# A first load of 16 rows, and the norm at the head of VectorE, in an attention and MLP kernel bound by its loads

## The chip, the cores and the metric

The kernel runs on one core of a Trainium2 chip. The metric is the device time of one execution in microseconds; the time before is the median of 3 runs. The profile is of one further execution, whose own time is given beside its span. An engine in the profile is PE (TensorE, matrix products; PEld is its loading of weights), DVE (VectorE), ACT (ScalarE), POOL (GpSimd) or SP (SyncE, which issues the loads here). Data come from HBM, the memory of the chip, into SBUF, the on-chip memory of 128 partitions, by 16 DMA engines.

## What is computed

A layer for one decoded token of 8 sequences: x plus grouped-query attention over a cache plus an MLP with the Mish activation, both on the normed x.

```python
xn = layernorm(x)                        # x: 8 x 1 x 512
q = (xn @ wq).reshape(8, 1, 32, 128)     # 32 query heads, 8 key heads
k, v = repeat(k_cache, 4), repeat(v_cache, 4)   # caches: 8 x 8 x 8192 x 128
p = softmax(q @ k.T * 128 ** -0.5)
attention = (p @ v) @ wo
h = xn @ w1 + b1                         # 512 -> 1792
mlp = (h * tanh(softplus(h))) @ w2
out = x + attention + mlp
```

All is float32. The two caches are 537 MB of the 561 MB that are read; each byte of them is used once.

## The kernel before

The caches are worked off in 32 units (`UNITS`), one for each sequence and each pair of key heads. A unit has one load of keys and one of values, each 128 rows of 64 KB (8.39 MB), one row to a partition of the large tile `kv`. Values have one place in it, `V_AT`; the two places of keys, `K_AT`, take turns and overlap by a half. The first keys are put into the place of the values. The weights of four units' queries, `wq`, come into the tile `ws`; `w1` comes into `kv` from `W1_AT` on, where x, its centred copy `xc`, the squares and a permuted copy `xd` lie at first.

The program is written as a list of operations for each engine. A class, `Program`, records them in the order in which the code names them, finds which must wait for which, and emits each engine's list in that order; middle units are folded into loops on VectorE and TensorE. Every emitted instruction has the one line of the emitter (L378), so that the profile is read by tiles. `tell` and `take` are marks handed from a giver to a taker. SP's list is nearly only loads, issued in order; each load waits until the last readers and writers of its place are through.

The head of the program, ahead of the first unit, runs as follows. ACT's queue issues x (8 rows of 2 KB) and b1. SP issues `wq` (`load_q`, lines 495 to 498) and the first keys (`load_unit`, lines 500 to 508). VectorE clears four PSUM banks, then makes small constant matrices out of an identity matrix (`perm`, `gsum`, `mask`, `wide`, `dsel`, `fsel` and others, lines 524 to 568), and after them norms x (lines 571 to 585), with the squares and a square root on ScalarE. TensorE first multiplies x into the bank `A`, where the result is gathered; then it turns the normed x (`xn4`), and turns it once more in another order for the hidden layer (`xnT`). `project` multiplies `xn4` with `wq` in two halves, each copied by ScalarE to `qp` and turned into `M`. VectorE masks the queries, `spread` multiplies them out into `qr`, and `key_weights` makes the weights `wk` for the scores. `scores` takes `wk` and the keys (32 matmuls into the bank `S`), `softmax` finds the maximum and the exponentials, `turn` puts them in the order that `values` needs. `hidden` (18 matmuls with `w1` and `b1`) stands behind the first unit's `turn`.

Loads behind the head: `w1` and the second keys are issued ahead of the first projection in the code; the first values wait for the first scores, since they go into the place of the first keys; from there keys and values alternate.

Of the kernel before, what the change touches and what calls it, by code (L numbers as in the profile page):

```python
# [9 lines left out]
F32 = mybir.dt.float32  # L10
# [4 lines left out]
P = 128  # L15
# [44 lines left out]
K_AT = (ROW, ROW + ROW // 2)  # L60
W1_AT = ROW
W2_AT = 2 * ROW
PLACES = 2 * ROW + ROW // 2


# [360 lines left out]
def kernel(  # L426
# [68 lines left out]
    def load_q(m):  # L495

        rows = wq.rearrange("j p f -> (j p f)").rearrange("(m p f) -> m p f", m=NP, p=P)
        nc.sync.dma_start(ws, rows[m]).tell("wq")
# [14 lines left out]
    nc.scalar.dma_start(x_sb, x)  # L513
    b1_sb = kv[:G, W1_AT + 7168 : W1_AT + 7168 + FG]
    nc.scalar.dma_start(b1_sb, b1.rearrange("(g f) -> g f", g=G))
    load_q(0)
    k_t = {0: load_unit(kT, 0, V_AT)}
    w1_t = kv[:, W1_AT : W1_AT + W1R * W1F].rearrange("p (i f) -> p i f", i=W1R)


    make_identity(nc, ident)
    nc.gpsimd.memset(ones, 1.0)
    nc.gpsimd.memset(pt8, 0.0)
    for t in (H, O, M, A):
        nc.vector.memset(t, 0.0)
    for d in range(2):
        nc.vector.tensor_copy(
            perm.rearrange("p (d k c h) -> p d k c h", d=2, c=2, h=REP)[:, d],
# [2 lines left out]
    nc.vector.reduce_sum(  # L531
        gsum, ident.rearrange("p (x g q) -> p g x q", g=4, q=PP), axis=AX.XY
    )
    nc.vector.reduce_sum(mask, ident.rearrange("p (x d) -> p x d", x=NB), axis=AX.X)
    nc.vector.reduce_sum(bsel, ident.rearrange("p (g q) -> p q g", g=G), axis=AX.X)
    nc.vector.reduce_sum(
        isel, ident.rearrange("p (c t h) -> p t c h", t=TL, h=H2), axis=AX.XY
# [1 line left out]
    for d in range(2):  # L539
# [2 lines left out]
            ident.rearrange("p (c d k h) -> p d h c k", c=2, d=2, h=REP)[:, d],  # L542
            axis=AX.XY,
        )
    nc.vector.reduce_sum(
        wide[:, 0], ident.rearrange("p (g i) -> p g i", g=DG), axis=AX.X
    )
    nc.vector.tensor_copy(
        wide[:, 1:], wide[:, 0:1].to_broadcast([P, NB - 1, DG])
    )  # L550
    nc.vector.reduce_sum(dsel, ident.rearrange("p (g i) -> p i g", i=DI), axis=AX.X)
    nc.vector.reduce_sum(
        fsel, ident.rearrange("p (c h g) -> p h c g", h=2, g=2 * W1R), axis=AX.XY
    )
    nc.vector.reduce_sum(usel, ident.rearrange("p (q i) -> p i q", i=WOR), axis=AX.X)
    nc.vector.reduce_sum(
        qsel[:, :Q], ident.rearrange("p (q i) -> p q i", i=WOR), axis=AX.X
# [9 lines left out]
        .to_broadcast([G, 2, 2, B]),  # L567
    )


    st = const.tile([B, 8], F32, name="st")
    nc.vector.reduce_sum(st[:, 0:1], x_sb, axis=AX.X)
    nc.vector.tensor_scalar_mul(st[:, 1:2], st[:, 0:1], 1.0 / D)
    nc.vector.tensor_scalar(xc, x_sb, st[:, 1:2], None, op0=ALU.subtract)
    nc.scalar.activation(sq, xc, AF.Square, accum_out=st[:, 2:3])
    nc.vector.tensor_scalar(
        st[:, 3:4], st[:, 2:3], 1.0 / D, EPS, op0=ALU.mult, op1=ALU.add
    )
    nc.scalar.activation(st[:, 4:5], st[:, 3:4], AF.Sqrt)
    nc.vector.reciprocal(st[:, 5:6], st[:, 4:5])  # L580
    nc.vector.tensor_mul(st[:, 6:7], st[:, 5:6], st[:, 5:6])
    nc.vector.tensor_mul(st[:, 7:8], st[:, 6:7], st[:, 3:4])
    nc.vector.tensor_scalar(st[:, 6:7], st[:, 7:8], -0.5, 1.5, op0=ALU.mult, op1=ALU.add)
    nc.vector.tensor_mul(st[:, 4:5], st[:, 6:7], st[:, 5:6])
    nc.vector.tensor_scalar(xc, xc, st[:, 4:5], None, op0=ALU.mult)
    nc.tensor.matmul(A[:B, :], ident[:B, :B], x_sb, start=True, stop=False)
    for c in range(CC):
        nc.tensor.transpose(M[:, c * B : (c + 1) * B], xc[:, c::CC], ident[:B, :B])
    nc.vector.tensor_copy(xn4.rearrange("p c b -> p (c b)"), M[:, 0:32])
    xd = kv[:B, W1_AT + 3 * D : W1_AT + 5 * D].rearrange("p (i k) -> p i k", i=W1R)  # L590
    for h in range(2):
        nc.vector.tensor_copy(
            xd.rearrange("p i (c h g) -> p h i c g", c=CC, h=2)[:, h],
            xc.rearrange("p (c g i) -> p i c g", c=CC, i=W1R),
        )
    for i in range(W1R):
        nc.tensor.transpose(
            M[:, 32 + i * B : 32 + (i + 1) * B], xd[:, i], ident[:B, :B]
        )
    for h in range(2):  # L600
        nc.vector.tensor_scalar(
            xnT[:, :, h],
            M[:, 32 : 32 + W1R * B].rearrange("p (i b) -> p i b", i=W1R),
            fsel[:, h : h + 1],
            None,
            op0=ALU.mult,
        )

    def project(m, qp):

        nc.tensor.take("wq")
        w = ws.rearrange("p (c f) -> p c f", c=CC)
        for d in range(2):
            for c in range(CC):
                nc.tensor.matmul(
                    H[:B, :],
                    xn4[:, c, :],
                    w[:, c, d * 512 : (d + 1) * 512],
                    start=(c == 0),
                    stop=(c == CC - 1),  # L620
                )
            nc.scalar.copy(qp[:B], H[:B]).tell("qp")
            nc.tensor.take("qp")
            for h in range(REP):
                at = 192 + (d * REP + h) * B
                made = nc.tensor.transpose(
                    M[:, at : at + B], qp[:B, h * DH : (h + 1) * DH], ident[:B, :B]
                )
        made.tell("tq")
        qT = ws[:, 2 * BW : 2 * BW + H2 * B]  # L630
        nc.vector.take("tq")
        nc.vector.tensor_scalar_mul(qT, M[:, 192 : 192 + H2 * B], DH**-0.5).tell("q")
        return qT
# [47 lines left out]
    def scores(j, k, first, part):  # L681

        if part == 0:
            nc.tensor.take("wk", f"k{j % 2}")
        w = wk
        lo = 0 if first else DI // 2
        kk = k.rearrange("p (i c f) -> p i c f", i=DI, c=HALF)
        for n in range(DI // 2):
            i = lo + n
            for c in range(HALF):  # L690
                made = nc.tensor.matmul(
                    S[64 * c : 64 * (c + 1), :],
                    w[:, i].rearrange("p d k h -> p (d k h)"),
                    kk[:, i, c, :],
                    start=(part == 0 and n == 0),
                    stop=(part == 1 and n == DI // 2 - 1),
                )
        if part == 1:
            made.tell("s")

    def softmax(j):
        nc.vector.take("s")
        nc.vector.relay()
        nc.vector.tensor_reduce(nm, S, axis=AX.X, op=ALU.max, negate=True).tell("nm")
        nc.tensor.take("nm")
        nc.tensor.transpose(M[:1, 0:P], nm, ident).tell("mt")
        nc.vector.take("mt")
        row = M[:1, 0:P].rearrange("p (c d k h) -> p d h c k", c=2, d=2, h=REP)
        for d in range(2):
            low_max = nc.vector.tensor_reduce(nr[:, d], row[:, d], axis=AX.XY, op=ALU.min)  # L710
        low_max.tell("nr")
        nc.vector.take("nr")
        for c in range(2):
            wide_max = nc.vector.tensor_copy(
                nx[:, c],
                nr.rearrange("p d (o h) -> p d o h", o=1).to_broadcast([1, 2, NH * G, REP]),
            )
        wide_max.tell("nx")
        nc.tensor.take("nx")
        nc.tensor.transpose(  # L720
            M[:, 128:129], nx.rearrange("p c d k h -> p (c d k h)"), ident[:1, :1]
        ).tell("xt")
        nc.vector.take("xt")
        nc.vector.tensor_copy(nmx, M[:, 128:129])
        nc.scalar.activation(es[j % 2], S, AF.Exp, bias=nmx, accum_out=l).tell("e")
# [97 lines left out]

    hp = H[:, :FG]

    def hidden(w1_t, b1_sb):
        for i in range(W1R):
            for n in range(2):
                nc.tensor.matmul(
                    hp[Q * n : Q * n + 2 * B, :],  # L830
                    xnT[:, i].rearrange("p h b -> p (h b)"),
                    w1_t[:, i, n * FG : (n + 1) * FG],
                    start=(i == 0),
                    stop=False,
                )
        for n in range(2):
            nc.tensor.matmul(
                hp[Q * n : Q * n + 2 * B, :],
                gsel[:, n].rearrange("p h b -> p (h b)"),
                b1_sb,  # L840
                start=False,
                stop=True,
            )
        for e in range(2):
            nc.vector.tensor_copy(
                hid[64 * e : 64 * (e + 1)], hp[:64, FG // 2 * e : FG // 2 * (e + 1)]
            )
# [85 lines left out]
    def down(lo, hi, w):  # L933
# [8 lines left out]
            )  # L942


    nc.sync.dma_start(
        kv[:, W1_AT : W1_AT + W1R * W1F],
        w1.rearrange("j p f -> (j p f)").rearrange("(p f) -> p f", p=P),
    )
    qT = project(0, es[0])
    k_t[1] = load_unit(kT, 1, K_AT[1])  # L950
    mask_queries(qT)
    spread()
# [4 lines left out]
    for j in range(UNITS):  # L957
# [14 lines left out]
        elif j > 0:  # L972
            k_t[j + 1] = load_unit(kT, j + 1, K_AT[(j + 1) % 2])
        scores(j, k, j % 2 == 0, 1)
        softmax(j)
        if b == 0 and j > 0:
            with nc.only("sums"):
                sums()
# [15 lines left out]
            load_q(j // B + 1)  # L994
        if more and b == MAKE_Q:
            with nc.only("make"):
                qT = project(j // B + 1, es[(j + 1) % 2])
                mask_queries(qT)
        turn(j, late)
        if j == 0:  # L1000
            hidden(w1_t, b1_sb)
        if j > 0:
            merge(j - 1)
    sums()
# [86 lines left out]
```

## Time and profile before

| | before |
|---|---|
| median of 3 runs | 1303.69 us (1303.64 to 1304.04) |
| time of the profiled execution | 1303.81 us |
| its span, first to last instruction | 1302.0 us |
| busy: PE, DVE, ACT, POOL | 912.2, 399.5, 43.1, 1.7 us |
| read from HBM | 561.01 MB |
| mean rate over the span | 431 GB/s |

Rows of a timeline begin with the start and the length in microseconds, then have engine, line, operation, output<-inputs, and shapes; in square brackets stands how long the engine was idle ahead of it and what ended that. Rows of stretches have the borders, then the busy time of each engine, the granted clock of TensorE as a share, the mean busy share of the DMA engines and the rate in GB/s. A transfer that is under way at a border is counted to one side, so that in short stretches the share can pass 1.

### The profile page before, as it was taken

How to read it: one execution, taken by the hardware profiler on the slowest of the kernel's cores; microseconds unless marked ns; L12 is line 12 of the kernel's file. 1: busy time of each engine (PE TensorE's matmuls, PEld its weight loads, DVE VectorE, ACT ScalarE, POOL GpSimd, SP SyncE). 2: the span in 40 equal slices, each digit the busy share in tenths (PEclk: the TensorE clock that was granted, in tenths of full speed). 3: DMA queues.
4: the chain of work that ended last, by engine and by line, in shares of the span. 5: the costliest groups of instructions: out<-in, count | busy, mean ns of one | idle time of the engine just before them, and what ended most of it. 6: DMA issues, size and time to landing. Idle time of an engine off the chain costs nothing. (4 is left out here: it accounts for less than half of the span.)

```text
span 1302.0 us, 11473 instructions
## 1 busy us (share of the span) xinstructions
PE 912.2 (70%) x4570; PEld 297.8 (23%) x4570; DVE 399.5 (31%) x874; ACT 43.1 (3%) x104; POOL 1.7 (0%) x8
## 2 busy tenths in 40 slices
PE   4877767668766668775678666677576667666667
PEld 1222222222222222222222222222222222222121
DVE  3332233431333331233321333322333331333431
ACT  2000000000000000000000000000000000000000
POOL 0000000000000000000000000000000000000000
PEclk9899778898788788888887877798887798788788
DMA  9999999999999999999999999999999999999998
GB/s 400 452 422 441 427 437 433 435 433 431 439 427 443 425 445 425 443 425 445 425 443 427 443 427 441 429 435 433 433 437 433 435 429 441 427 443 425 443 418 351
DMA packets 11555, 561.22 MB, mean 431 GB/s; under 512 B 1292, under 2 KB 1552, under 8 KB 1944
## 3 DMA queue, kind: packets, MB, share of 16 engines
q1 hardware_dynamic: 11520, 561.06, 99.6%
q8 instruction: 6, 0.10, 0.0%
q14 instruction: 5, 0.04, 0.0%
q10 hardware_dynamic: 24, 0.02, 0.0%
HBM read 561.01 MB, written 0.07 MB: 431 GB/s over the span
## 5 line engine op out<-in xcount | busy, mean ns | idle before, releaser
L378 PE MATMUL s<-kv,wk 128*64 128x512 f32 x2048 | 515.7, 667 | 226.2 <-PEq L365 226.2
L378 PEld LDWEIGHTS s<-kv,wk 128*64 128x64 f32 x2048 | 174.5, 154 | 550.0 <-issue 550.0
L378 PE MATMUL o<-kv,pt 128*32 128x512 f32 x2048 | 268.1, 683 | 22.7 <-PEq L365 22.3
L378 DVE TENSOR_REDUCE nm<-s 128x1 f32<-128x512 f32 x32 | 22.1, 692 | 479.5 <-DVEq L365 479.5
L378 PEld LDWEIGHTS o<-kv,pt 128*32 128x32 f32 x2048 | 81.5, 123 | 183.1 <-issue 182.7
L378 DVE TENSOR_SCALAR os<-o,isel 128x128 f32<-128x128 f32 x32 | 11.2, 351 | 287.7 <-DVEq L365 287.7
L378 DVE STREAM_TRANSPOSE tr<-x 128x512 f32<-128x512 f32 x128 | 80.0, 682 | 1.3 <-DVEq L365 1.3
L378 DVE TENSOR_TENSOR wk<-qr,mask 128x512 f32<-128x512 f32 x64 | 61.8, 1007 | 8.9 <-DVEq L365 6.4
L378 DVE SCALAR_TENSOR_TENSOR pt<-tr,gsum,y 64x256 f32<-64x256 f32 x128 | 56.2, 479 | 5.2
L378 ACT ACTIVATE e<-s,nmx 128x512 f32<-128x512 f32 x32 | 22.0, 687 | 1046.1 <-DVE nmx L378 1046.1
L378 DVE SCALAR_TENSOR_TENSOR y<-tr,gsum,y 128x512 f32<-128x512 f32 x64 | 48.3, 755 | 9.4
L378 DVE SCALAR_TENSOR_TENSOR os<-o,isel,os 128x128 f32<-128x128 f32 x96 | 33.7, 351 | 14.1 <-DVEq L365 0.3
L378 PE MATMUL x<-e,perm 128*128 128x512 f32 x64 | 36.5, 653 | 1.4 <-PEq L365 1.3
L378 PE MATMUL m<-ident,nm 128*1 128x128 f32 x32 | 8.6, 269 | 32.2 <-PEq L365 32.2
L378 PE MATMUL h<-ws,xn 128*8 128x512 f32 x64 | 30.5, 622 | 0.0
L378 PE MATMUL m<-ident,nx 1*128 1x1 f32 x32 | 6.4, 200 | 34.2 <-PEq L365 34.2
L378 PE MATMUL t<-ident,os 128*128 128x128 f32 x32 | 9.6, 299 | 26.6 <-PEq L365 26.6
L378 DVE TENSOR_SCALAR y<-tr,gsum 128x512 f32<-128x512 f32 x32 | 24.1, 754 | 1.2
L378 DVE TENSOR_REDUCE nr<-m 1x4 f32<-1x64 f32 x64 | 11.0, 207 | 18.1 <-DVEq L365 18.1
L378 PEld LDWEIGHTS m<-ident,nm 128*1 128x1 f32 x32 | 2.5, 79 | 59.5 <-issue 59.5
L378 PEld LDWEIGHTS x<-e,perm 128*128 128x128 f32 x64 | 10.0, 192 | 24.1 <-issue 23.7
L378 PEld LDWEIGHTS t<-ident,os 128*128 128x128 f32 x32 | 4.5, 140 | 46.6 <-issue 46.6
(91 smaller groups left out, 154.1 us busy)
## 6 DMA issues: line engine op xcount, KB each, us to landing
ws<-in_wq SPq DMA_DIRECT2D x4, 2048.0 KB, 32.6
kv<-in_wo SPq DMA_DIRECT2D x4, 2048.0 KB, 24.4
kv<-in_w SPq DMA_DIRECT2D x1, 3584.0 KB, 22.0
kv<-in_w SPq DMA_DIRECT2D x2, 1024.0 KB, 32.0
kv<-in_w SPq DMA_DIRECT2D x2, 512.0 KB, 33.8
kv<-in_kT SPq DMA_DIRECT2D x32, 29.1
kv<-in_v SPq DMA_DIRECT2D x32, 29.4
kv<-in_w SPq DMA_DIRECT2D x1, 384.0 KB, 34.7
```

The lines of the kernel that those rows point to most:

```text
L378: ins = getattr(engine, op.method)(*[here(x) for x in op.args], **{k: here(x) for k, x in op.kw.items()})
```

## The change

Four things are changed in the head.

The first keys' load is cut in two on SP: 16 rows (`HEAD_ROWS`) are issued first, then `wq`, then the other 112 rows. TensorE's first score matmul takes the mark `k0` twice, once for each part. `w1` and the second keys are recorded behind the projection, no longer ahead of it.

SP's list, before and now; rows name the tile, the tensor that is loaded and the rows by elements of 4 bytes. Before:

```order
L378 DMA ws<-in_wq 128x4096
L378 DMA kv<-in_kT 128x16384
L378 DMA kv<-in_w 128x7168 [waits at_tensor]
L378 DMA kv<-in_kT 128x16384
L378 DMA kv<-in_v 128x16384 [waits past_vector]
```

Now:

```order
L379 DMA kv<-in_kT 16x16384
L379 DMA ws<-in_wq 128x4096
L379 DMA kv<-in_kT 112x16384
L379 DMA kv<-in_w 128x7168 [waits at_tensor]
L379 DMA kv<-in_kT 128x16384
L379 DMA kv<-in_v 128x16384 [waits past_vector]
```

One load has become two around `wq`; `w1` and the second keys have kept their places in the list, but `w1` waits for another instruction of TensorE.

VectorE norms x ahead of nearly all the constants. ScalarE takes a square root of one element of the identity at the start, so that its table is there.

VectorE from its start; `st` holds the sums of the norm, `kv<-kv,st` are steps on x itself, `m` and `h` are banks. Before:

```order
L378 MEMSET h 128x512
L378 MEMSET o 128x512
L378 MEMSET m 128x512
L378 MEMSET a 128x512
L378 COPY perm<-ident 128x64 x2
L378 TENSOR_REDUCE gsum<-ident 128x4
L378 TENSOR_REDUCE mask<-ident 128x16
L378 TENSOR_REDUCE bsel<-ident 128x32
```

Now:

```order
L379 MEMSET m 128x512
L379 TENSOR_REDUCE st<-kv 8x1
L379 TENSOR_SCALAR st<-st 8x1
L379 TENSOR_SCALAR kv<-kv,st 8x512
L379 MEMSET h 128x512
L379 TENSOR_REDUCE dsel<-ident 128x16
L379 TENSOR_SCALAR st<-st 8x1
L379 TENSOR_REDUCE wide<-ident 128x8
L379 RECIPROCAL st<-st 8x1
```

The norm stood behind some twenty rows of constants and is now at the second row, with constants between its steps and behind it.

TensorE makes both halves of the first projection in two banks, turns x for the hidden layer while ScalarE copies, and only then turns the queries; the matmul of x into `A` comes behind that. The 18 matmuls of the hidden layer are spread over the first softmax.

TensorE up to the first scores (`s`); `e_90` and `e_91` hold the copied queries. Before:

```order
L378 MATMUL a<-kv,ident 8x512
L378 MATMUL m<-ident,kv 128x8 x12
L378 MATMUL h<-ws,xn_82 8x512 x4
L378 MATMUL m<-ident,e_90 128x8 x4
L378 MATMUL h<-ws,xn_82 8x512 x4
L378 MATMUL m<-ident,e_90 128x8 x4
L378 MATMUL h<-ws,wide 128x512
L378 MATMUL y<-ws,wide 128x512
L378 MATMUL s<-kv,wk 64x512 x32
```

Now:

```order
L379 MATMUL m<-ident,kv 128x8 x4
L379 MATMUL h<-ws,xn_82 8x512 x4
L379 MATMUL y<-ws,xn_82 8x512 x4
L379 MATMUL x<-ident,kv 128x8 x8
L379 MATMUL m<-ident,e_90 128x8 x4
L379 MATMUL m<-ident,e_91 128x8 x4
L379 MATMUL a<-kv,ident 8x512
L379 MATMUL h<-ws,wide 128x512
L379 MATMUL y<-ws,wide 128x512
L379 MATMUL s<-kv,wk 64x512 x32
```

The matmul `a<-kv,ident`, the last reader of x, moved from the first row to behind the projection.

The diff, cut to its core:

```diff
+HEAD_ROWS = 16
...
-    load_q(0)
-    k_t = {0: load_unit(kT, 0, V_AT)}
+    k_t = {0: kv[:, V_AT : V_AT + ROW]}
+    k_rows = kT[:NB].rearrange("j p f -> (j p f)").rearrange("(p f) -> p f", p=P)
+    nc.sync.dma_start(k_t[0][:HEAD_ROWS], k_rows[:HEAD_ROWS]).tell("k0")
+    load_q(0)
+    nc.sync.dma_start(k_t[0][HEAD_ROWS:], k_rows[HEAD_ROWS:]).tell("k0")
...
-    for t in (H, O, M, A):
-        nc.vector.memset(t, 0.0)
+    st = const.tile([B, 8], F32, name="st")
+    nc.scalar.activation(st[:, 0:1], ident[:B, :1], AF.Sqrt)
+    nc.vector.memset(M, 0.0)
+    nc.vector.reduce_sum(st[:, 0:1], x_sb, axis=AX.X)
...
-    nc.tensor.matmul(A[:B, :], ident[:B, :B], x_sb, start=True, stop=False)
...
-    def project(m, qp):
+    def project(m, qps, banks, fill=None):
...
+        products(0)
+        if fill is not None:
+            products(1)
+            fill()
+            turned(0)
+        else:
+            turned(0)
+            products(1)
+        turned(1).tell("tq")
...
         if part == 0:
             nc.tensor.take("wk", f"k{j % 2}")
+            if j == 0:
+                nc.tensor.take("k0")
...
+    qT = project(0, es, (H, Y), turn_x)
+    nc.tensor.matmul(A[:B, :], ident[:B, :B], x_sb, start=True, stop=False)
     nc.sync.dma_start(
         kv[:, W1_AT : W1_AT + W1R * W1F],
         w1.rearrange("j p f -> (j p f)").rearrange("(p f) -> p f", p=P),
     )
-    qT = project(0, es[0])
     k_t[1] = load_unit(kT, 1, K_AT[1])
...
-        softmax(j)
+        if j == 0:
+            softmax(j, hidden)
+            hidden(4, 6)
+        else:
+            softmax(j)
...
         if j == 0:
-            hidden(w1_t, b1_sb)
+            hidden(6, W1R)
```

More of the change, by code (lines that the diff above doesn't have):

```diff
@@ L523 @@
     nc.gpsimd.memset(pt8, 0.0)
-    for t in (H, O, M, A):
-        nc.vector.memset(t, 0.0)
+    st = const.tile([B, 8], F32, name="st")
+    nc.scalar.activation(st[:, 0:1], ident[:B, :1], AF.Sqrt)
+    nc.vector.memset(M, 0.0)
+    nc.vector.reduce_sum(st[:, 0:1], x_sb, axis=AX.X)
+    nc.vector.tensor_scalar_mul(st[:, 1:2], st[:, 0:1], 1.0 / D)
+    nc.vector.tensor_scalar(xc, x_sb, st[:, 1:2], None, op0=ALU.subtract)
+    nc.scalar.activation(sq, xc, AF.Square, accum_out=st[:, 2:3])
+    nc.vector.memset(H, 0.0)
+    nc.vector.reduce_sum(dsel, ident.rearrange("p (g i) -> p i g", i=DI), axis=AX.X)
+    nc.vector.tensor_scalar(
+        st[:, 3:4], st[:, 2:3], 1.0 / D, EPS, op0=ALU.mult, op1=ALU.add
+    )
+    nc.scalar.activation(st[:, 4:5], st[:, 3:4], AF.Sqrt)
+    nc.vector.reduce_sum(
+        wide[:, 0], ident.rearrange("p (g i) -> p g i", g=DG), axis=AX.X
+    )
+    nc.vector.reciprocal(st[:, 5:6], st[:, 4:5])
+    nc.vector.tensor_mul(st[:, 6:7], st[:, 5:6], st[:, 5:6])
+    nc.vector.tensor_mul(st[:, 7:8], st[:, 6:7], st[:, 3:4])
+    nc.vector.tensor_scalar(st[:, 6:7], st[:, 7:8], -0.5, 1.5, op0=ALU.mult, op1=ALU.add)
+    nc.vector.tensor_mul(st[:, 4:5], st[:, 6:7], st[:, 5:6])
+    nc.vector.tensor_scalar(xc, xc, st[:, 4:5], None, op0=ALU.mult)
+    for c in range(CC):
+        nc.tensor.transpose(M[:, c * B : (c + 1) * B], xc[:, c::CC], ident[:B, :B])
+    nc.vector.tensor_copy(xn4.rearrange("p c b -> p (c b)"), M[:, 0:32])
+    nc.vector.tensor_copy(
+        wide[:, 1:], wide[:, 0:1].to_broadcast([P, NB - 1, DG])
+    )
+    nc.vector.reduce_sum(mask, ident.rearrange("p (x d) -> p x d", x=NB), axis=AX.X)
+    xd = kv[:B, W1_AT + 3 * D : W1_AT + 5 * D].rearrange("p (i k) -> p i k", i=W1R)
+    for h in range(2):
+        nc.vector.tensor_copy(
+            xd.rearrange("p i (c h g) -> p h i c g", c=CC, h=2)[:, h],
+            xc.rearrange("p (c g i) -> p i c g", c=CC, i=W1R),
+        )
+    nc.vector.reduce_sum(
+        fsel, ident.rearrange("p (c h g) -> p h c g", h=2, g=2 * W1R), axis=AX.XY
+    )
+    nc.vector.memset(A, 0.0)
+    nc.vector.memset(O, 0.0)
     for d in range(2):
@@ L533 @@
     )
-    nc.vector.reduce_sum(mask, ident.rearrange("p (x d) -> p x d", x=NB), axis=AX.X)
     nc.vector.reduce_sum(bsel, ident.rearrange("p (g q) -> p q g", g=G), axis=AX.X)
@@ L544 @@
         )
[L545 to L554, printed above, removed]
     nc.vector.reduce_sum(usel, ident.rearrange("p (q i) -> p i q", i=WOR), axis=AX.X)
@@ L568, with products @@
     )
[L571 to L585, printed above, removed]
-    nc.tensor.matmul(A[:B, :], ident[:B, :B], x_sb, start=True, stop=False)
[L587 to L607, printed above, removed]
-    def project(m, qp):
+    def project(m, qps, banks, fill=None):
         nc.tensor.take("wq")
         w = ws.rearrange("p (c f) -> p c f", c=CC)
-        for d in range(2):
+        def products(d):
             for c in range(CC):
                 nc.tensor.matmul(
-                    H[:B, :],
+                    banks[d][:B, :],
                     xn4[:, c, :],
@@ L621, in project, with turned @@
                 )
-            nc.scalar.copy(qp[:B], H[:B]).tell("qp")
+            nc.scalar.copy(qps[d][:B], banks[d][:B]).tell("qp")
+        def turned(d):
             nc.tensor.take("qp")
@@ L626, in project @@
                 made = nc.tensor.transpose(
-                    M[:, at : at + B], qp[:B, h * DH : (h + 1) * DH], ident[:B, :B]
+                    M[:, at : at + B], qps[d][:B, h * DH : (h + 1) * DH], ident[:B, :B]
                 )
-        made.tell("tq")
+            return made
+        products(0)
[7 more added lines that the diff above has]
+        turned(1).tell("tq")
         qT = ws[:, 2 * BW : 2 * BW + H2 * B]
@@ L699, in scores, with softmax @@
             made.tell("s")
-    def softmax(j):
+    def softmax(j, fill=lambda lo, hi: None):
         nc.vector.take("s")
@@ L704, in softmax @@
         nc.vector.tensor_reduce(nm, S, axis=AX.X, op=ALU.max, negate=True).tell("nm")
+        fill(0, 2)
         nc.tensor.take("nm")
@@ L718, in softmax @@
         wide_max.tell("nx")
+        fill(2, 4)
         nc.tensor.take("nx")
@@ L824, with hidden @@
     hp = H[:, :FG]
-    def hidden(w1_t, b1_sb):
-        for i in range(W1R):
+    def hidden(lo, hi):
+        for i in range(lo, hi):
             for n in range(2):
@@ L835, in hidden @@
                 )
+        if hi < W1R:
+            return
         for n in range(2):
@@ L942, in down, with turn_x @@
             )
+    def turn_x():
+        for i in range(W1R):
+            nc.tensor.transpose(X[:, i * B : (i + 1) * B], xd[:, i], ident[:B, :B])
+        for h in range(2):
+            nc.vector.tensor_scalar(
+                xnT[:, :, h],
+                X[:, : W1R * B].rearrange("p (i b) -> p i b", i=W1R),
+                fsel[:, h : h + 1],
+                None,
+                op0=ALU.mult,
+            )
+    qT = project(0, es, (H, Y), turn_x)
+    nc.tensor.matmul(A[:B, :], ident[:B, :B], x_sb, start=True, stop=False)
     nc.sync.dma_start(
@@ L996 @@
             with nc.only("make"):
-                qT = project(j // B + 1, es[(j + 1) % 2])
+                qT = project(j // B + 1, [es[(j + 1) % 2]] * 2, (H, H))
                 mask_queries(qT)
```

## The prediction

> **What bounds the kernel now.** I read the strip of forty slices first, then the chain of work that ended last, then single stretches of the span.
>
> ```profile
> DMA  9999999999999999999999999999999999999998
> 1263.61 34.75 DMA kv<-in_w
> 1298.40 0.74 PE h L378 x15
> 1299.16 0.29 DVE os L378
> ```
>
> The first row is the mean busy share of the 16 DMA engines in each fortieth of the span, in tenths: full everywhere. The other three (start, length, what) are the end of the chain: nearly 35 us of waiting for one load, then about 1 us of work on it. Busy engines do not prove that none of them waits, so I cut the span where the loads begin and end.
>
> ```profile
> core 0: us, PE busy (x) PEld busy (x) DVE busy (x) ACT busy (x) POOL busy (x), PEclk, DMA share, GB/s
> 1.80:1.98 0.18, 0.00 (x0) 0.00 (x0) 0.18 (x1) 0.15 (x1) 0.18 (x2) 1.00 0.19 68
> 2.00:3.00 1.00, 0.00 (x0) 0.00 (x0) 0.89 (x3) 1.00 (x1) 0.70 (x1) 1.00 1.08 217
> 3.00:4.00 1.00, 0.70 (x1) 0.10 (x2) 1.00 (x7) 0.11 (x1) 0.00 (x0) 1.00 0.78 295
> 4.00:5.00 1.00, 1.00 (x2) 0.00 (x0) 0.97 (x7) 0.00 (x0) 0.00 (x0) 1.00 0.99 426
> 27.00:1294.00 1267.00, 894.92 (x4464) 292.84 (x4468) 388.67 (x837) 37.93 (x96) 0.00 (x0) 0.84 1.00 434
> 1294.00:1302.00 8.00, 4.23 (x72) 1.32 (x64) 0.29 (x1) 0.58 (x1) 0.00 (x0) 0.93 0.33 124
> ```
>
> The last two columns matter. From 27 to 1294 us the DMA share is 1.00 at 434 GB/s, with no hole; all engines of computation have slack (TensorE is busy 895 of 1267 us). Before that, two microseconds carry little: at 2 to 3 and 3 to 4 us the rate is 217 and 295. So the time is one sum: when the loads start, plus bytes over rate, plus a tail of some 4 us behind the last byte. An edit matters only if it moves the start, lowers the rate, or lets the queue run empty. The span is 1302.0 us, the profiled execution 1303.81, which is 0.12 over the median of 1303.69; I sum against 1303.81.
>
> **The change part by part.** First, does the queue stay full when the order of the head is turned over?
>
> ```profile
> 0.90 0.59 ACTq L378 DMA_DIRECT2D kv<-in_x  x1
> 0.95 0.38 SPq L378 DMA_DIRECT2D ws<-in_wq  x1
> 1.39 0.42 SPq L378 DMA_DIRECT2D kv<-in_kT  x1
> 14.40 0.33 SPq L378 DMA_DIRECT2D kv<-in_w  x1
> 14.77 0.43 SPq L378 DMA_DIRECT2D kv<-in_kT  x1
> 49.92 0.33 SPq L378 DMA_DIRECT2D kv<-in_v  x1
> 71.28 0.33 SPq L378 DMA_DIRECT2D kv<-in_kT  x1
> ws<-in_wq SPq DMA_DIRECT2D x1, 2048.0 KB, 7.6
> kv<-in_w SPq DMA_DIRECT2D x1, 3584.0 KB, 22.0
> ```
>
> These are the issues (start, length), and for two of them KB and us to landing. wq is 2.10 MB, each load of keys or values 8.39 MB (128 rows of 64 KB), w1 3.67 MB. With a start at 2.0 and 0.8 us lost in the ramp, wq and the first keys keep the engines busy until 2.8 + 10.49 MB / 434 GB/s = 27.0 us; w1 and the second keys until 54.8; the first values until 74.1. The next issues come at 14.4, 49.9 and 71.3: early each time, by 12.6, 4.9 and 2.8 us.
>
> In the changed kernel w1 must wait for more of TensorE's row, since x and its copies lie where w1 lands and their last reader is now the 8x512 matmul behind the projection; the second keys stand behind w1 on SP. The chain up to there:
>
> ```profile
> 6.29 0.67 DVE L378 TENSOR_REDUCE st<-kv 8x1 f32<-8x512 f32 x1
> 8.41 1.28 ACT L378 ACT_TABLE_LOAD   x1
> 12.06 0.19 DVE L378 COPY xn<-m 128x32 f32<-128x32 f32 x1 [0.73 <-PE m L378]
> 3.29 1.87 PE L378 MATMUL a<-kv,ident 8*8 8x512 f32 x2 [3.29 <-DVE a L378]
> 13.35 1.02 PE L378 MATMUL m<-ident,kv 8*128 8x8 f32 x8 [1.33 <-DVE kv L378]
> 14.29 5.33 PE L378 MATMUL h<-ws,xn 128*8 128x512 f32 x8
> 20.69 3.60 PE L378 MATMUL h<-ws,xn 128*8 128x512 f32 x8
> 25.05 0.38 PE L378 MATMUL m<-ident,e 8*128 8x8 f32 x4 [0.76 <-PEq L365]
> 33.36 16.38 PE L378 MATMUL s<-kv,wk 128*64 128x512 f32 x64 [3.00 <-PEq L365]
> ```
>
> The norm now takes 12.25 - 6.29 = 5.96 us, a table load of 1.28 included. Moved to the head of VectorE it starts when x is there (by 3.29, when the matmul on x ran) and when the early square root is through, at about 3.4; the constants that stood ahead of it go behind it, and the second table load leaves the chain. xn is then ready at 3.4 + 5.96 - 1.28 = 8.1 instead of 12.25. The two memsets and reductions put among the norm's steps lie in its waits for ScalarE. wq now comes one packet later per engine: landed at 0.95 + 7.6 + 1.05 MB / 434 (2.4) = 11.0. So the projection starts at 11.0, not 14.29. Its two products take 5.33 + 3.60, the eight turns of x 1.02, the two turns of queries 0.76, the matmul on x 1.87: w1 is issued at 23.6, still 3.4 us ahead of the end of the queue at 27.0, and the second keys right behind. Data follow an issue after about 1 us (0.95 to 2.0). So the later w1 costs nothing, with 2.4 us to spare; each microsecond beyond that would cost one. The scores then wait for both loads of k0 rather than for the weights; the weights come some 3.7 us sooner (the last turn of queries ends at 11.0 + 10.7 = 21.7, not 25.4), so where k0 is on time v0 and k2 are issued that much sooner and gain slack, and where k0 is late the whole queue is late with it. All the rearranged work on VectorE, TensorE and ScalarE is thus worth **nothing**: the full queue hides it. w1's parts of the hidden layer now stand between the steps of the first softmax; w1 lands 8.5 us behind k0, inside the 16.38 us of scores.
>
> What is left is the queue itself. **Start.** The ramp at 2 to 4 us lacks 217 + 139 KB, 0.82 us at 434. [...] Between 0 and -0.8 us; I take the middle, -0.4. The extra issue (0.4 us on SP) and its completion packets lie under the first packets, at nothing.
>
> **First load (T1).** 16 rows of 64 KB go to partitions 0 to 15 alone. At full rate that is 1.05 MB / 434 = 2.4 us, and costs nothing, as these bytes were to be moved anyhow. But no big load in this trace is narrower than 128 partitions, and 434 GB/s over 128 partitions may be a limit of the engines (27 each) or of the places that take the data (3.4 for each partition). If the rate went by partitions, 16 of them would take 54 GB/s: 19.3 us, +16.9, and wq and all else would stand behind it in every engine's queue. These are the ends. The nearest row is the stretch 1.80 to 1.98: there only x is under way, on 8 partitions, at 68 GB/s, 8.5 for each partition. At that, 16 partitions take 136 GB/s: 7.7 us, **+5.3**. I take it, being the only narrow load seen; it is a stretch of start-up, so a loose guide.
>
> [...]
>
> **Third load (T2).** 112 rows, seven for each engine, 16.9 us at 434. [...] If all goes on at an engine's own pace: +0. If the rate follows the share of partitions, 112/128 of 434 gives 19.3 us, +2.4. If every packet shares its place with another: +16.9. Between 2.4 and 16.9, far apart and with no row nearer, I take the geometric middle, **+6.4**; it goes with T1, since both come from a limit on the side that takes the data.
>
> Sum: 1303.8 + 5.3 + 6.4 - 0.4 = **1315.1**, say 1315.
>
> **The rivals.** (a) *Narrow loads run at full pace*: the limit is the engines' 27 GB/s each. For it: 434 in the long stretch whatever the load. Then T1 and T2 are nothing and the time is 1303.8 - 0.4 = 1303.4 (1303.0 to 1304.0): not slower. It decides as soon as the first load is done by about 5 us. The same time comes out if the change doesn't do what it says, that is if the 16 rows go to few engines and those get fewer of the 112: each still has eight rows of k0. [...] (b) *Lockstep*: the 112 rows are dealt out so that all engines always write 16 neighbouring rows, seven times over; then each step costs what the first load costs: 8 x 5.3 = 42, 1346. Against it: loads of 128 rows show no such crowding. (c) *The queue runs empty* since w1 is late: it needs the projection's chain to slip by over 2.4 us with T1 at nothing; it would cost 1 to 3 us, 1304.4 to 1306.4.
>
> **How the numbers follow.** Forecast 0.55, (a) 0.34, (b) 0.07, (c) 0.04. The long stretch cannot tell engines from partitions; I lean to the partitions because the one narrow load seen moved at 68 where eight engines at 27 would give 217. The forecast's own range is 1306 (T1 and T2 near their low ends) to 1323 (T1 16.9 with T2 2.4). The range takes in (a) and these: 1302.9 to 1323, leaving out (b) and a tenth of the forecast's cases, where both terms are high. Runs of this kernel tell about 0.2%, 2.6 us, from no change. Faster by that: 0.03, taken out of (a), as the whole ramp holds only 0.8 us. Within it: the rest of (a), 0.31, and 0.03 of (c): 0.34. Slower: the forecast, (b) and the rest of (c): 0.63.
>
> **What would show it.** Forecast: DMA rate far under 434 between 3 and 10 us, wq landing after 14 us rather than 11, a rate under 434 until some 38 us, then 434 as before. (a): 430 from 3 us on and w1 issued near 23.6. (b): a low rate until 60 us and more. (c): a stretch near 27 us with an empty queue. Wrong above all if the places that take data have room for one engine per partition.

## The result, and the profile after

The changed kernel takes 1324.03 us (median of 4 runs, 1323.57 to 1324.47) against 1303.74 before (by now also 4 runs): 20.3 us slower, a ratio of 1.0156 with a 95% interval of 1.0143 to 1.0168. The time lies 1 us above the range of the prediction. The profiled execution took 1323.98 us, with a span of 1322.2.

The strip of forty slices of the changed kernel: the busy share of the DMA engines in tenths, and the rate in GB/s.

```profile
DMA  9999999999999999999999999999999999999998
GB/s 247 336 439 421 436 440 428 432 442 426 436 440 426 434 440 436 426 438 438 426 436 438 430 432 440 428 434 442 426 434 440 428 434 438 438 426 436 439 420 347
```

The first of these rows is the same as before and would hide everything: the engines are busy from the first slice on. The second row has the answer. In the first two slices (66 us) the rate is 247 and 336 where it was 400 and 452; from the third to the last but one both stay between 418 and 445. So a busy share near 1 does not mean full pace. Cut at the borders of the loads:

```profile
core 0: us, PE busy (x) PEld busy (x) DVE busy (x) ACT busy (x) POOL busy (x), PEclk, DMA share, GB/s
2.00:11.30 9.30, 0.65 (x4) 0.55 (x4) 6.59 (x25) 2.22 (x5) 0.70 (x1) 1.00 1.03 131
11.30:16.60 5.30, 0.00 (x0) 0.00 (x0) 1.59 (x8) 0.00 (x0) 0.00 (x0) 1.00 0.84 352
16.60:46.00 29.40, 13.24 (x38) 3.48 (x38) 3.85 (x6) 3.60 (x5) 0.00 (x0) 0.83 1.03 254
46.00:1314.00 1268.00, 886.71 (x4464) 291.32 (x4464) 386.71 (x834) 35.47 (x93) 0.00 (x0) 0.85 1.00 433
```

The stretch of the first load has 131 GB/s (a part of it is wq's first packets), that of wq (128 rows again) 352 (without those), that of the 112 rows 254, and everything behind has 433. The packet records of the trace (start, length and size of each transfer) say the same: each of the 16 rows took 7.9 to 9.2 us, where a packet of 64 KB took 2.42 us in the kernel before, while wq's packets came down to 0.61 us, as before. At 434 the 112 rows would have been through in 16.9 us; they take some 30. The issues and landings of the changed kernel say the same; in the last three rows the last number is us from issue to landing, of the 16 rows, of wq, and of the 112 rows.

```profile
0.95 0.39 SPq L379 DMA_DIRECT2D kv<-in_kT  x1
1.40 0.41 SPq L379 DMA_DIRECT2D ws<-in_wq  x1
1.86 0.63 SPq L379 DMA_DIRECT2D kv<-in_kT  x1
29.28 0.34 SPq L379 DMA_DIRECT2D kv<-in_w  x1
...
65.46 0.33 SPq L379 DMA_DIRECT2D kv<-in_v  x1
85.94 0.33 SPq L379 DMA_DIRECT2D kv<-in_kT  x1
...
kv<-in_kT SPq DMA_DIRECT2D x1, 11.8
...
ws<-in_wq SPq DMA_DIRECT2D x1, 2048.0 KB, 16.4
...
kv<-in_kT SPq DMA_DIRECT2D x1, 47.6
```

The engines of computation, in the timeline of the changed kernel:

```profile
8.02 0.19 DVE L379 COPY xn<-m 128x32 f32<-128x32 f32 x1 [0.74 <-PE m L379]
...
17.96 5.77 PE L379 MATMUL h<-ws,xn 128*8 128x512 f32 x8 [9.97 <-PEq L366]
28.23 1.02 PE L379 MATMUL a<-kv,ident 8*8 8x512 f32 x2
49.62 15.66 PE L379 MATMUL s<-kv,wk 128*64 128x512 f32 x64 [17.47 <-PEq L366]
```

The norm does what it was moved for: xn is ready at 8.2 us, not 12.25. But the projection then waits 10 us for wq, and the scores 17.5 us for the keys. At the other end the chain is as it was, 35.30 us of waiting for the last load against 34.75:

```profile
1283.20 35.30 DMA kv<-in_w
```

### The profile page after: what moved, and what is told of

It is laid out like the page before. It is cut to its first block, busy times and chain, and to the rows that moved or that the text cites. A ratio compares the mean times of both kernels' runs of the same rounds, so it can differ in the third digit from the quotient of the medians.

```text
span 1322.2 us, 11475 instructions
## 1 busy us (share of the span) xinstructions
PE 903.9 (68%) x4570; PEld 296.7 (22%) x4570; DVE 399.5 (30%) x874; ACT 42.1 (3%) x104; POOL 1.7 (0%) x8
## 5 line engine op out<-in xcount | busy, mean ns | idle before, releaser
L379 PE MATMUL h<-ws,xn 128*8 128x512 f32 x56 | 27.4, 635 | 10.0 <-PEq L366 10.0
## 6 DMA issues: line engine op xcount, KB each, us to landing
ws<-in_wq SPq DMA_DIRECT2D x4, 2048.0 KB, 33.8
```

The source lines that it names most:

```text
L379: ins = getattr(engine, op.method)(*[here(x) for x in op.args], **{k: here(x) for k, x in op.kw.items()})
```

## The experiments

Theory at the outset: all of the loss lies in the two loads that are narrower than 128 partitions, on the side that takes the data. Rivals: the new order of the head has a share in it; narrow loads are slow for their source, for their number of rows, or as they come first.

**Which half of the change.** One kernel keeps everything but the split of the first keys, one has nothing but the split.

```diff
 # e1_rest_only: the changed kernel
-    k_t = {0: kv[:, V_AT : V_AT + ROW]}
...
-    nc.sync.dma_start(k_t[0][:HEAD_ROWS], k_rows[:HEAD_ROWS]).tell("k0")
     load_q(0)
-    nc.sync.dma_start(k_t[0][HEAD_ROWS:], k_rows[HEAD_ROWS:]).tell("k0")
+    k_t = {0: load_unit(kT, 0, V_AT)}
...
-            if j == 0:
-                nc.tensor.take("k0")
 # e2_split_only: the kernel before
+    k_t = {0: kv[:, V_AT : V_AT + ROW]}
...
+    nc.sync.dma_start(k_t[0][:HEAD_ROWS], k_rows[:HEAD_ROWS]).tell("k0")
     load_q(0)
-    k_t = {0: load_unit(kT, 0, V_AT)}
+    nc.sync.dma_start(k_t[0][HEAD_ROWS:], k_rows[HEAD_ROWS:]).tell("k0")
...
+            if j == 0:
+                nc.tensor.take("k0")
```

> The changed kernel with the first keys in one load of 128 rows behind wq, as before; all the rest of the change stays. Theory (the loss is all in the two narrow loads): 1303.3 to 1303.9 us, no change against 1303.7, with wq landed near 9 us and w1 issued near 22 us, ahead of the end of the queue at 27. Rival (a good part of the 20 us comes from the order of the head, as w1 and the second keys are issued at 29 instead of 14 us): 1306 us or more, with a stretch near 27 us in which the DMA engines stand idle.

> The kernel before with nothing but the split load (16 rows, wq, 112 rows). Theory: the whole loss, 1323 to 1325 us, with the 112 rows at about 250 GB/s as in the changed kernel. Rival (order of the head matters): clearly under 1322 us.

Without the split: 1303.77 us (11 runs) against 1303.82, ratio 1.0 (0.9991 to 1.0009). With the split alone: 1324.02 (4 runs), ratio 1.0154 (1.0138 to 1.0171), with 250 GB/s in the stretch from 16.6 to 46 us, where the changed kernel has 254. The split is the whole loss; the new order of the head is worth nothing that can be measured, either way. A stretch of e1_rest_only, and its issues of w1 and of the first values:

```profile
4.00:27.00 23.00, 13.39 (x42) 3.97 (x42) 11.43 (x38) 4.53 (x8) 0.00 (x0) 0.97 1.00 434
```

```profile
19.48 0.33 SPq L379 DMA_DIRECT2D kv<-in_w  x1
...
44.37 0.33 SPq L379 DMA_DIRECT2D kv<-in_v  x1
```

w1 is issued 5 us later than before (19.5; 22 was expected) and the first values 5.5 us earlier, and neither shows, as the queue is full on both sides of them (434 GB/s from 27 to 1294 us as well).

**The same split, cut the other way.** The first load has the same 1.05 MB, but an eighth of the columns of all 128 rows.

```diff
 # e3_columns: the changed kernel
-    nc.sync.dma_start(k_t[0][:HEAD_ROWS], k_rows[:HEAD_ROWS]).tell("k0")
+    nc.sync.dma_start(k_t[0][:, : ROW // 8], k_rows[:, : ROW // 8]).tell("k0")
     load_q(0)
-    nc.sync.dma_start(k_t[0][HEAD_ROWS:], k_rows[HEAD_ROWS:]).tell("k0")
+    nc.sync.dma_start(k_t[0][:, ROW // 8 :], k_rows[:, ROW // 8 :]).tell("k0")
```

> The changed kernel, but the first keys are cut by columns and not by rows: first 128 rows of 2048 elements (the same 1.05 MB), then wq, then 128 rows of the other 14336. Theory (only the narrow set of partitions costs): 1303.5 to 1304.2, no change against before, the 20 us gone. Rival (two loads for one, or wq in second place, cost): over 1306.

It takes 1303.43 us (10 runs) against 1303.58, ratio 0.9998 (0.9989 to 1.0008): no difference. So neither the further load nor wq's second place costs anything. This is the way to have a piece of the keys first, and it does not beat the kernel before by an amount that can be told: what it could win is the ramp of the start alone, 0.8 us at 434 GB/s.

**The narrow loads by themselves.** The kernel before gets one load more ahead of wq, into the place of the second keys, which overwrite it later. The result stays what it was; there is 1.05 MB more to move (7.34 MB in p112), worth 2.4 us (16.9) at 434 GB/s. The probes of eight rows have half of the 1.05 MB; the estimate for them is 2.4 us all the same, for one packet of 64 KB (2.42 us in the kernel before) on each of eight engines. The rows come from the start of the first keys unless the table says otherwise (p112: rows 16 to 127).

```diff
 # the kernel before; the slices of the probes stand in the table
+    k_rows = kT[:NB].rearrange("j p f -> (j p f)").rearrange("(p f) -> p f", p=P)
+    spare = kv[:, K_AT[1] : K_AT[1] + ROW]
+    nc.sync.dma_start(spare[0:16], k_rows[0:16])
     load_q(0)
```

> The kernel before with one load more ahead of wq: the first 16 rows of the keys into partitions 0 to 15 of the place of the second keys, which are loaded over it later. At full rate the 1.05 MB cost 2.4 us: 1306.1. Theory (neighbouring partitions share a way in): the first load takes as long as in the changed kernel, 2.4 + 6.6 = 9.0 us more than before: 1312.7. Rival (the slow first load there was start-up or wq's place behind it): 1306 to 1308.

> The same as p16_step1, same 16 rows of HBM, but into partitions 0, 7, 14 and so on to 105. Theory (which partitions take the data decides, neighbours share a way in): well under p16_step1, with packets of mostly 2.4 us and the longest about 4.8: 1306 to 1309 us. Rival (a load of 16 rows is slow for its source or for its number of rows, or the rate goes by the number of partitions, 16 here as there): as p16_step1, 1312.7 us or more. [...]

> The kernel before with one load more ahead of wq: rows 16 to 127 of the first keys into partitions 16 to 127 of the place of the second keys. Theory (the third load of the change is slow by itself, without the first or wq around it): 7.34 MB in about 30 us as there, 1334. At an engine's full pace 16.9 us, 1320.7; by the share of partitions 19.3, 1323.1. Rival (it was slow there since the first load had put the engines out of step): 1321 to 1324.

> As p16_step7, with the same partitions 0, 7 to 105, but the rows of HBM are 0, 7 to 105 as well, 448 KB apart and not 64. Theory (the side that takes the data decides): 1308.2 as there. Rival (neighbouring rows of HBM are in each other's way): 1306.2.

> [...]

> As p16_step7, but into partitions 18, 25, 32 and so on to 123. [...]

> [...] Rival (a load of fewer than 128 rows pairs engines and places badly however they lie, or the step decides): 1308.3 as with start 0.

> [...]

> The kernel before with one load more ahead of wq: 8 rows of keys (64 KB each) into partitions 0, 4, 8 to 28. If each of eight engines takes one row at its full pace, these engines are 2.4 us later than before: 1306.2. The load into 16 partitions seven apart cost 4.5 us, twice the full pace on all 16 engines. [...]

> As p8_own, but into partitions 4, 8 to 32, one group further. [...]

> [...]

> [...] Time 1306.4 to 1308.5.

Each of these was run once. The rate is that of the stretch that is read below. The extra time is against the run of the kernel before beside it.

| probe | partitions | GB/s, 5.3 to 6.6 us | us to landing | time, us | extra, us |
|---|---|---|---|---|---|
| p16_step1 | 0:16 | 0 | 11.9 | 1312.86 | 9.0 |
| p16_step8 | 0:121:8 | 0 | 7.9 | 1308.65 | 5.0 |
| p16_step7 | 0:106:7 | 0 | 7.6 | 1308.25 | 4.4 |
| p16_src7 | 0:106:7, rows of HBM 0:106:7 | 67 | 8.2 | 1308.50 | 4.9 |
| p16_from10 | 10:116:7 | 0 | 8.0 | 1308.51 | 4.7 |
| p16_from18 | 18:124:7 | 346 | 8.9 | 1308.45 | 4.8 |
| p16_from11 | 11:117:7 | 407 | 5.6 | 1306.69 | 2.9 |
| p8_own | 0:29:4 | 407 | | 1306.38 | 2.8 |
| p8_next | 4:33:4 | 409 | | 1306.55 | 3.0 |
| p8_pair | 0:36:5 | 370 | | 1306.36 | 2.7 |
| p8_two | 0:22:3 | 101 | | 1308.53 | 4.8 |
| p112 | 16:128 | | 33.8 | 1333.48 | 29.9 |

The two loads of the change are slow by themselves: p16_step1 costs 9.0 us, 6.6 over its bytes, and p112 costs 29.9, 13.0 over them. Together 19.6 of the 20.3 us.

Width is not the cause. p16_from11 has 16 rows, as p16_step1, and the step of p16_step7, and costs 2.9 us, little more than the 2.4 that its bytes are worth. One partition lower (p16_from10) the same load costs 4.7. The source is not the cause either: p16_src7 reads other rows of HBM into the partitions of p16_step7 and takes about as long. What decides is which partitions take data at the same time: 16 rows cost 9.0 us in 16 neighbours, 5.0 at a step of eight, and at a step of seven 4.4 to 4.9 from partitions 0, 10 and 18 but 2.9 from 11. Nor is a load slow for having fewer than 128 rows: at half pace eight rows would cost 4.8 us by estimate (twice 2.4), and p8_own cost 2.8 and p8_next 3.0; at a step of three, p8_two cost 4.8. The partitions of the probes were chosen by an assumption of the author's on which of them get in each other's way; no run shows a rule for that.

The stretches show how the probes differ: from 5.3 to 6.6 us a load at full pace is nearly through and wq is under way (the last column is GB/s). First p16_from11, which cost 2.9 us:

```profile
5.30:6.60 1.30, 0.00 (x0) 0.00 (x0) 1.26 (x7) 0.00 (x0) 0.00 (x0) 1.00 0.98 407
```

Then p16_from18, which cost 4.8:

```profile
5.30:6.60 1.30, 0.00 (x0) 0.00 (x0) 1.27 (x7) 0.00 (x0) 0.00 (x0) 1.00 0.93 346
```

And p16_from10, which cost 4.7:

```profile
5.30:6.60 1.30, 0.00 (x0) 0.00 (x0) 1.26 (x7) 0.00 (x0) 0.00 (x0) 1.00 0.00 0
```

In p16_from11 wq runs; the 16 rows took 2.6 to 3.2 us each by the packet records. In p16_from18 most engines are on wq too, and only two rows are late (4.7 and 6.1 us, the other 14 2.4 to 3.4); the later one sets the landing, 8.9 us. In p16_from10 not one engine begins a packet in that stretch (packets are counted where they begin): all 16 are still on their first row, which took 4.0 to 4.95 us each. p16_step7 has the same zeros; p16_src7, with the same partitions, is less even (3.4 to 5.7 us, and 67 GB/s in this stretch). So at one and the same step two rows may be late, or all, or none. In p8_two even wq's packets beside the eight rows are slow. Here is the stretch from 4.0 to 5.3 us, first of p8_own (2.8 us extra), then of p8_two (4.8):

```profile
4.00:5.30 1.30, 1.16 (x2) 0.00 (x0) 1.27 (x8) 0.00 (x0) 0.00 (x0) 1.00 0.50 190
4.00:5.30 1.30, 1.16 (x2) 0.00 (x0) 1.27 (x8) 0.00 (x0) 0.00 (x0) 1.00 0.50 101
```

In both, half of the engines (DMA share 0.50) begin packets of wq, and these move 190 GB/s in p8_own and 101 in p8_two (0.61 to 0.77 us for 16 KB in the one, 1.28 to 1.30 in the other); the eight rows of p8_two took 4.2 to 4.9 us, all of them. In p8_pair two of the eight rows took 4.1 and 5.1 us and the others 2.6 to 3.2, and the stretch from 5.3 to 6.6 us has 370:

```profile
5.30:6.60 1.30, 0.00 (x0) 0.00 (x0) 1.27 (x7) 0.00 (x0) 0.00 (x0) 1.00 0.87 370
```

The 112 rows show both patterns. Their packets are taken here in order of start, 16 at a time, which makes seven sets. The stretches of p112 at the borders of these sets (first two, next two, last three):

```profile
1.90:11.10 9.20, 1.87 (x2) 0.10 (x2) 6.62 (x29) 3.41 (x5) 0.81 (x1) 1.00 1.04 229
11.10:17.90 6.80, 1.66 (x12) 1.48 (x12) 1.94 (x6) 0.00 (x0) 0.00 (x0) 1.00 1.03 309
17.90:31.40 13.50, 0.00 (x0) 0.00 (x0) 0.00 (x0) 0.00 (x0) 0.00 (x0) 1.00 1.02 233
```

229, 309 and 233 GB/s: about half of the 434 in the first and last stretch, better in the one between. The packet records bear it out: in the third and fourth set two of the 16 packets took 4.4 to 4.95 us and the other 14 3.15 to 3.6; in the five other sets all took 4.0 to 5.7. The 112 rows of the changed kernel show the same pattern (14 at 2.8 to 3.6 us and two at 4.4 to 4.7 in the third and fourth set). Against 2.42 us at full pace, the other 14 packets were thus mostly slowed too in these sets, while p16_from18 had them at 2.4 to 3.4. Which rows an engine takes isn't shown; neither the views nor the records name the engine of a packet.

Three things stay open: why all rows are late in p16_from10 and p8_two and only two in p16_from18 and p8_pair; why in the 112 rows the other 14 packets of a set with two late ones are slowed more than in p16_from18; and why the late pair of p8_pair doesn't show in its time (1306.36, with 1306.38 in p8_own) while that of p16_from18 does. The engines need not end together: in the kernel before, the last 16 packets of 64 KB ended between 1267.3 and 1270.2 us, so that a late packet on an early engine may hide. Whether it was on one isn't on record.

## Why the prediction was right in direction and wrong in size

What bounds the kernel: right. The time moved by what the queue lost in its first 46 us, and the long stretch behind it ran at 433 GB/s as before.

The queue stays full with w1 behind the projection: right. In e1_rest_only the stretch from 4 to 27 us has 434 GB/s, and time and order of the head part company. The xn of the forecast, 8.1 us, was 8.2. In e3_columns, where the loads go at full pace with wq second (442 GB/s from 4 to 27 us), w1 was issued at 22.84 us (forecast of rival (a): 23.6).

Start, -0.4 us: no run shows this term. By the packet records the first packet from SP began at 2.00 us in the changed kernel and at 1.99 before, and neither e1_rest_only nor e3_columns differs from before by what a measurement can tell.

First load (T1), +5.3: the side that takes the data is right, and the size is near, 6.6 in p16_step1, but that is luck. The price came from the stretch with x, 68 GB/s, read as what eight partitions take. The same row has a DMA share of 0.19: the engines were mostly idle. By the packet records x's packets of 2 KB took 0.081 to 0.098 us, 21 to 25 GB/s each, near the 27 of an engine at full pace (64 KB in 2.42 us), so that row shows no limit. Nor do 16 partitions as such set a pace, as p16_from11 shows with 2.9 us.

Third load (T2), +6.4: **this is the step that failed.** It measured 13.0 alone. The term was bounded at +2.4 and +16.9, and for want of a row I took the geometric middle. That choice amounts to some packets meeting another and most not; the runs showed all 16 packets at 4.0 to 5.7 us, against 2.42, in five sets of seven, and 14 at 3.15 to 3.6 in the other two (p112), so that nearly the upper end was due. With 6.6 and 13.0 in place of the two terms, and nothing for the start, the sum would have been 1323.4. Hence also the range: it had T1 at its top with T2 at its bottom, and not T2 near its top with T1 as taken, which is what came. The low rate lasted to 46 us, not to some 38 as forecast.

Rivals: (a), narrow loads at full pace, is refuted for these partitions (p16_step1, 6.6 us over the bytes' worth) and nearly true for others (p16_from11, 0.5 over). (b), the lockstep of 16 neighbours, would have been 42 us, seven eighths of it, 37, in the third load; p112 shows 13. (c), an empty queue, didn't come up. The 16 neighbours of p16_step1 went at near a quarter of the pace: 6.6 us over the bytes' worth, where a quarter would be 7.3 by estimate (three times 2.42).

## What to carry to other kernels

A load that is cut by rows keeps its bytes but may lose its pace: in these runs the partitions that were written at the same moment decided (16 rows cost 2.9 us or 9.0), and the "busy" row of the DMA engines didn't show it (a share of 1.03 at 254 GB/s); read the rate beside it. Cut by columns over all 128 partitions instead: here that cost nothing (1303.43 us against 1303.58). Where loads bound this kernel and the queue was never empty, reordering the engines' work at the head bought nothing (1303.77 against 1303.82).

## What the runs showed that was not expected

Slowness did not always stay with a few packets. In p16_from18 only two packets were late (4.7 and 6.1 us), but in the 112 rows the 14 others of such a set were slowed as well (3.15 to 3.6 us in p112). In p16_from10 all 16 rows took 4.0 to 4.95 us, and in p8_two all eight rows were late and wq's packets beside them slow (101 GB/s on half of the engines, where p8_own has 190). And 16 rows on 16 partitions can go near full pace if they are well placed: 11, 18 to 116 cost 2.9 us, 10, 17 to 115 cost 4.7.
